# Half an item later: when the first network's side work reads another engine's result

## Chip, core and metric

The kernel runs on one core of a Trainium2 chip. The metric is device time in microseconds (us) of one execution. Before the change it is 1354.57 us, the median of three runs (1351.06, 1354.57 and 1358.54). The work of the core is done by five engines that run side by side and meet only where one waits for another: TensorE (PE, matmuls; PEld is its weight load), VectorE (DVE), ScalarE (ACT), GpSimd (POOL) and SyncE (SP), which issues most DMAs. Each engine takes its own instructions strictly in the order in which they were written for it.

## What is computed

A gated linear attention, then two feed-forward networks on 3072 tokens (4 batches x 768 positions):

```python
for t in range(S):                                  # q, k, v, alpha: [4, 8, 768, 48]
    state = alpha[:, :, t, :, None] * state + einsum('bhd,bhe->bhde', k[:, :, t], v[:, :, t])
    y[:, :, t] = einsum('bhd,bhde->bhe', q[:, :, t], state)
x = y as [3072, 384]
...
h = x @ w_in                                        # first network, 384 -> 2048 -> 384
x = where(h > 0, h, exp(min(h, 0)) - 1) @ w_out
...
p = domain_probs / (domain_probs.sum(-1) + 1e-9)    # second network, 4 experts, 384 -> 1024 -> 384
out = sum_e p[:, e] * (maximum(x @ w1[e], 0) @ w2[e])
```

## The kernel before

**Pieces.** The positions are cut into 6 chunks of 128; a chunk of all 4 batches gives 512 columns. A (chunk, batch) pair is an attention *unit*. Every fp32 operand of a big matmul is held as two fp32r parts, the rounded value ("hi", an ACT copy) and the rest ("lo", a DVE subtraction that reads hi); `split` makes both. A product is then three matmuls: hi·hi, hi·lo, lo·hi.

**First network.** It is a list of 96 *items* (chunk, slice of 128 hidden rows): the first 8 slices of chunk 0, all 16 of chunk 1, the other 8 of chunk 0, and then 16 each of chunks 2 to 5. Item i runs on the engines as

- `first` (9 matmuls, L420) into one of three PSUM banks h0 to h2, below "first matmuls of item i";
- `elu`: two ACT activations (L429, L430) and one DVE operation (L431), in place in the bank;
- `second` of item i-2 (9 matmuls, L446), which reads the parts `g` of item i-2;
- `parts`: an ACT copy (L436, below G0) and a DVE subtraction (L437, below G1). G1 is the last to read the bank, so the bank is free again only after it.

**Side work.** Beside the items run: the attention of the next chunk (steps of `unit_steps`: scores L250 and their mask L258, transposed keys L271 with an ACT copy L277, the prefix products P L205 and their inverse by logarithm and exponentials L213 to L215, Newton step L228 to L230, q times P L240, output L307/L314, state L341 with decay L351/L353); the way of the attention's output into the next chunk's x (`yout_t`'s `pack`: ACT copy L322, two DMAs to DRAM L324, one back L326, then `xtrans` splits it into x); the conversion of the first network's slices from 64-bit words (`conv_f64`: ACT multiply L406, three DVE bit operations L78, L81, L84, then a split into `w_W`); and the preparation of the second network's weights (`prep_w`: sums L474, splits into `wh`, DMAs to `wad` and `wbd`).

**What sets the order.** PE, ACT, DVE and POOL take the order in which the program writes them. `slots` puts steps behind the first matmuls of an item (half 0) or behind the second ones (half 1), `post` at the item's end. `later(f)` puts a follow-up (a mask, a lo part, a store) into a queue, and `flush` writes out what is in it:

```python
h = first(items[i])
self.flush()
... steps of half 0 ...
self.elu(h)
self.flush()
... second(items[i - 2]), steps of half 1, post ...
gs[items[i]] = self.parts(h)
```

Besides these two places, `do`, which runs each step, flushes the queue ahead of its step. SP's order is made by the scheduler. Two PSUM banks a0 and a1 serve the attention in turn: the scores of a unit need both, so they wait for the copy L322 and the decay L351 of the unit before, besides the DVE product L240.

Of the kernel before, what the change touches and what calls it, by code (L numbers as in the profile page):

```python
# [8 lines left out]
F32 = mybir.dt.float32  # L9
# [3 lines left out]
ALU = mybir.AluOpType  # L13
AX = mybir.AxisListType

B, H, S, D = 4, 8, 768, 48
# [72 lines left out]
class _Fast:  # L89
# [207 lines left out]
    def yout_t(self, u):  # L297


        nc = self.nc  # L300
        c, b = u
# [9 lines left out]
        for a in range(NP):  # L311
            for j in range(2):
                h = 2 * a + j
# [6 lines left out]
        def pack():  # L320
            y = self.ap.tile([128, NP * C], F32, tag="y", name="yt")
            nc.scalar.copy(y[0:SW], ps[0:SW])  # L322
            for j in range(2):
                nc.scalar.dma_start(out=self.x0d[b][D * j:D * (j + 1)], in_=y[64 * j:64 * j + D])  # L324
            x = self.ap.tile([128, KD, C], F32, tag="y", name="xr")
            nc.sync.dma_start(  # L326
                out=x, in_=self.x0d[b].rearrange("(k r) (a t) -> (r a) k t", k=KD, a=NP)
            )
            self.y[u] = x
# [67 lines left out]
    def conv_f64(self, f):  # L397
        nc = self.nc
# [9 lines left out]
        def bits():  # L408
            _f64_bits(nc, t, raw)
            self.split(w[:, 0, f % 2], w[:, 1, f % 2], tf)  # L410

# [21 lines left out]
    def parts(self, h):  # L433
        nc = self.nc
        g = self.hp.tile([128, 2, 512], F32R, tag="g", name="g")
        nc.scalar.copy(g[:, 0], h)  # L436
        nc.vector.tensor_tensor(out=g[:, 1], in0=h, in1=g[:, 0].bitcast(F32), op=ALU.subtract)  # L437
        return g
# [13 lines left out]
    def prep_w(self, g, nxt):  # L452
# [17 lines left out]
        def tile_w():  # L470
            return self.wp.tile([128, 3, 2, 128], F32R, tag="cv", name="wh", bufs=4)
# [4 lines left out]
        def end(c, q):  # L476
            t = tile_w()
            self.split(t[:, :, 0], t[:, :, 1], c)
            self.later(lambda: nc.sync.dma_start(out=self.wad[g][:, 3 * q:3 * q + 3], in_=t.bitcast(F32)))

# [4 lines left out]
        lo = lambda t, i, m=1: t[:, i:i + m] if m > 1 else t[:, i]  # L485
        tile_c = lambda: self.wp.tile([128, 3, 128], F32, tag="wc", name="wc", bufs=2)
        bc = lambda v, m: v.unsqueeze(1).to_broadcast([128, m, 128])
# [33 lines left out]
        def q4():  # L521
            t = tile_w()
            a = st[0][:, 1, 128:384].rearrange("p (n d) -> p n d", n=2)
            self.split(t[:, 0:2, 0], t[:, 0:2, 1], a)
            c = tile_c()
            tt(c[:, 0], w(1, 1), st["u"], sub)
            self.split(t[:, 2, 0], t[:, 2, 1], c[:, 0])
            self.later(lambda: nc.sync.dma_start(
                out=self.wbd[g][:, 0:768], in_=t.bitcast(F32).rearrange("p n h d -> p (n h d)")
            ))  # L530

# [10 lines left out]
        if nxt:  # L542
            s[5] += [nxt]
        return (load, (0,)), s
# [253 lines left out]
    def run(self):  # L798
# [22 lines left out]
        def do(step):  # L821
            if self.queue is not None:
                self.flush()
            for f, a in step:
                f(*a)
# [42 lines left out]
        for c in range(1, NCH):  # L868
# [3 lines left out]
            for n, s in enumerate(steps):  # L872
                k = av[n * len(av) // len(steps)]
                slots.setdefault(k, []).append(s)
                if n % 6 == 5:
                    slots[k].append([(load_next, ())])
            slots.setdefault((end - 1, 0), []).append([(self.xtrans, ((c, B - 1),))])

# [10 lines left out]
        for f in range(FS, F1):  # L889
            at((FS - 2, FS)[f - FS] if f < FS + 2 else f + 2, self.conv_f64, f)  # L890
            if f + 2 < F1:
                at(f + 2, self.load_f64, f + 2)
        b5 = n1 - F1
        at(b5 - 1, open_p2)
        at(FS + 4, self.load_probs)
# [7 lines left out]
        for n, s in enumerate(wsteps):  # L903
            at(w0 + n * (w1 - w0) // len(wsteps), do, s)
        for m in range(2):
# [45 lines left out]
        for i in range(n1):  # L951
# [10 lines left out]
            for f, a in post.pop(i, []):  # L962
                do([(f, a)])
            gs[items[i]] = self.parts(h)
        self.flush()
        self.queue = None
# [241 lines left out]
```

## Time and profile before

| | us |
|---|---|
| median of 3 runs | 1354.57 |
| profiled execution, its own time | 1352.57 |
| its span, first to last instruction | 1350.9 |
| PE busy | 1266.0 (94%) |
| DVE busy | 896.0 (66%) |
| ACT busy | 585.4 (43%) |
| POOL busy | 519.9 (38%) |
| mean granted TensorE clock | 0.974 |

The profiled execution lies 2.0 us below the median, and its own time is 1.7 us above its span. PE is the busiest engine, so what counts is where it is not busy or runs at less than its full clock. The page's 40 slices of the span show both at its start: PE is under nine tenths busy in six of the first nine slices (304 us), and its clock under nine tenths of full in five of the first seven (236 us); of the other 31 slices PE is under nine tenths busy in the last alone. The first network's items run from 42.5 to 602.6 us.

### The profile page before, as it was taken

To read this page: it belongs to the slowest core of one execution; us is meant where nothing else is said; L and a number is where in the kernel's file an instruction comes from. 1 tells how busy PE (TensorE), PEld (TensorE's weight loads), DVE (VectorE), ACT (ScalarE), POOL (GpSimd) and SP (SyncE) were. 2 spreads that over 40 slices of the span, in tenths; PEclk is the share of its full clock that TensorE was granted. 3 is DMA by queue.
4 is the path that set the end of the run, shared out by engine and by line. 5 is a ranking of instruction groups with operands and counts; after the bars stand their busy time and mean duration, and the time that the engine had idled before them with its cause. 6 is when DMAs were issued, how large, how long until landed. Compare 5 with 4: busy or idle time off the path is not lost.

```text
span 1350.9 us, 17707 instructions
## 1 busy us (share of the span) xinstructions
PE 1266.0 (94%) x6457; PEld 1022.5 (76%) x6457; DVE 896.0 (66%) x1513; ACT 585.4 (43%) x1076; POOL 519.9 (38%) x405
## 2 busy tenths in 40 slices
PE   8767979989999999999999999999999999999997
PEld 6546767767777778877887888778878878888886
DVE  7775676676667675656666675757676666667664
ACT  5444555555556655654434323243423332324231
POOL 0000000000000000457887664697865565547472
PEclk8788998999999999999999999999999999999999
DMA  5441424745466554682756546766463585434332
GB/s 218 170 152 65 140 92 174 234 158 199 141 208 196 190 181 156 213 294 91 278 195 229 179 176 215 296 254 251 163 258 123 198 314 179 168 129 169 127 102 77
DMA packets 71823, 248.28 MB, mean 184 GB/s; under 512 B 6712, under 2 KB 38296, under 8 KB 62384
## 3 DMA queue, kind: packets, MB, share of 16 engines
q1 hardware_dynamic: 68160, 237.62, 49.9%
q10 hardware_dynamic: 3568, 9.44, 1.9%
q8 instruction: 53, 0.87, 0.3%
q14 instruction: 42, 0.34, 0.1%
HBM read 182.89 MB, written 64.14 MB: 183 GB/s over the span
## 4 chain that ended last, share of the span: by engine, by line
PE 62%; DVE 15%; ACT 9%; issue 5%; POOL 4%; DMA 4%; ACTq 0%; SPq 0%; DVEq 0%; POOLq 0%
PE h L711 21%; PE t L761 12%; PE a L761 9%; PE h L420 7%; PE t L446 5%; PE h L761 4%; ACT g L436 2%; DVE P L205 2%; DVE u L731 2%; DVE h L431 1%; ACT wh L375 1%; DVE sm L258 1%; PE a L250 1%; ACT e L430 1%; DVE cv L84 1%
## 5 line engine op out<-in xcount | busy, mean ns | idle before, releaser
L420 PE MATMUL h<-x,w_W 128*128 128x512 f32 x864 | 228.3, 409 | 25.9 <-DVE g L437 16.6
L731 DVE TENSOR_TENSOR u<-h,u 128x512 f32<-128x512 f32 x258 | 177.5, 688 | 88.9 <-PE h L711 87.9
L446 PE MATMUL t<-g,w_W 128*128 128x512 f32 x864 | 219.3, 397 | 6.7 <-ACT g L436 3.5
L711 PE MATMUL h<-xc_Q,wa 128*128 128x512 f32 x780 | 219.4, 391 | 4.9 <-DVE c L731 2.4
L556 POOL TENSOR_TENSOR xs<-xr 128x512 f32<-128x512 f32 x8 | 10.3, 1294 | 544.1 <-ACT x1raw L937 544.1
L420 PEld LDWEIGHTS h<-x,w_W 128*128 128x128 f32 x864 | 167.4, 197 | 68.3 <-DVE g L437 20.0
L691 POOL TENSOR_TENSOR g_W<-c,g_W 128x512 fp32r<-128x512 f32 x128 | 164.8, 1303 | 121.8 <-ACT c L690 103.7
L689 ACT ACTIVATE g_W<-c 128x512 fp32r<-128x512 f32 x128 | 80.0, 626 | 272.0 <-DVE c L731 158.5
L446 PEld LDWEIGHTS t<-g,w_W 128*128 128x128 f32 x864 | 161.9, 190 | 46.0 <-DVE g L437 5.5
L711 PEld LDWEIGHTS h<-xc_Q,wa 128*128 128x128 f32 x780 | 145.6, 188 | 38.3 <-DVE u L731 4.3
L761 PE MATMUL t<-g_W,wb 128*128 128x512 f32 x576 | 157.6, 389 | 0.0
L437 DVE TENSOR_TENSOR g<-h,g 128x512 fp32r<-128x512 f32 x96 | 66.3, 691 | 89.8 <-ACT g L436 89.8
L761 PEld LDWEIGHTS t<-g_W,wb 128*128 128x128 f32 x576 | 108.0, 188 | 22.6 <-POOL g_W L691 0.2
L690 ACT ACTIVATE c<-c 128x512 f32<-128x512 f32 x192 | 121.1, 632 | 7.4
L731 DVE TENSOR_TENSOR c<-u,h 128x512 f32<-128x512 f32 x123 | 84.1, 686 | 50.3 <-PE h L711 37.1
L711 PE MATMUL h<-xc_W,wa 128*128 128x512 f32 x390 | 110.2, 391 | 5.1 <-DVE u L731 3.1
L725 DVE COPY u<-h 128x512 f32<-128x512 f32 x99 | 68.1, 691 | 66.7 <-PE h L711 66.4
L761 PE MATMUL a<-g_W,wb 128*128 128x512 f32 x384 | 111.7, 389 | 0.3 <-POOL g_W L691 0.3
L691 POOL TENSOR_TENSOR g_X<-c,g_X 128x512 fp32r<-128x512 f32 x64 | 82.7, 1304 | 62.6 <-ACT c L690 52.0
L689 ACT ACTIVATE g_X<-c 128x512 fp32r<-128x512 f32 x64 | 40.0, 626 | 142.5 <-DVE c L731 78.4
L431 DVE SCALAR_TENSOR_TENSOR h<-e,h 128x512 f32<-128x512 f32 x96 | 66.5, 693 | 44.6 <-ACT e L430 44.2
L711 PEld LDWEIGHTS h<-xc_W,wa 128*128 128x128 f32 x390 | 72.7, 188 | 22.6 <-DVE u L731 4.4
(139 smaller groups left out, 1948.1 us busy)
## 6 DMA issues: line engine op xcount, KB each, us to landing
wa<-wad SPq DMA_DIRECT2D x33, 1536.0 KB, 6.8
wb<-wbd SPq DMA_DIRECT2D x30, 1536.0 KB, 7.0
raw<-in_att_dram SPq DMA_DIRECT2D x22, 960.0 KB, 5.5
wad<-wh SPq DMA_DIRECT2D x44, 384.0 KB, 2.7
wbd<-wh SPq DMA_DIRECT2D x43, 384.0 KB, 3.4
xcd<-xh SPq DMA_DIRECT2D x30, 512.0 KB, 3.0
wraw<-in_wm_dram SPq DMA_DIRECT2D x16, 768.0 KB, 4.2
wraw<-in_we_dram SPq DMA_DIRECT2D x20, 576.0 KB, 4.6
```

What stands on the lines that cost most here:

```text
L205: nc.vector.tensor_tensor_scan(P[:, a, :], raw[:, A0 + a * C:A0 + (a + 1) * C], self.plo.to_broadcast([128, C]), 1.0, ALU.mult, ALU.max,)
L420: nc.tensor.matmul(h[:, 0:n], w[:, wl, fi, k * 128:(k + 1) * 128], x[:, xl, k, n0:n0 + n], start=(k == 0 and i == 0), stop=(k == KD - 1 an ...
L431: nc.vector.scalar_tensor_tensor(out=h, in0=e, scalar=-1.0, in1=h, op0=ALU.add, op1=ALU.max)
L437: nc.vector.tensor_tensor(out=g[:, 1], in0=h, in1=g[:, 0].bitcast(F32), op=ALU.subtract)
L446: nc.tensor.matmul(self.xa[k][:, 0:n], w[:, wl, fi, DM + k * 128:DM + (k + 1) * 128], g[:, gl, 0:n], start=(first and i == 0), stop=(last ...
L689: nc.scalar.activation(out=g[:, n, 0], in_=v, func=AF.Relu)
L690: nc.scalar.activation(out=v, in_=v, func=AF.Relu)
L691: nc.gpsimd.tensor_tensor(out=g[:, n, 1], in0=v, in1=g[:, n, 0].bitcast(F32), op=ALU.subtract)
L711: nc.tensor.matmul(b, w[:, wl], x[:, xl], start=(j == 0), stop=(j == 2))
L725: nc.vector.tensor_copy(out, b)
L731: (nc.vector if "b" in (a0, a1) or dst == "S5" else nc.gpsimd).tensor_tensor(out=out, in0=val(a0, b), in1=val(a1, b), op=ALU.add if op == ...
L761: nc.tensor.matmul(oa[m, d], wt[:, f, wl, d * 128:(d + 1) * 128], G[m][:, f, gl], start=first, stop=last)
```

## The change

Six edits, all in the first network's stretch and its side work:

1. `do` no longer flushes. Follow-ups now come out at two places in an item alone: behind its first matmuls and behind `elu`.
2. `parts` puts the G1 subtraction at the head of the queue, so it comes out behind the next item's first matmuls; nothing else stands on DVE between the old and the new place.
3. The splits of `conv_f64` and of `prep_w` (`end`, `q4`) go into the queue themselves, so that hi is written one flush behind the operation that makes its source, and lo one flush behind hi. The tiles `wc` have 4 buffers in place of 2.
4. The weight preparation's steps go into half items in place of item ends, and its next load one step later.
5. `xtrans` of a chunk's last unit goes half an item earlier.
6. The two stores of `pack` are issued by SP, not ACT.

```diff
@@ yout_t / pack
-                nc.scalar.dma_start(out=self.x0d[b][D * j:D * (j + 1)], in_=y[64 * j:64 * j + D])
+                nc.sync.dma_start(out=self.x0d[b][D * j:D * (j + 1)], in_=y[64 * j:64 * j + D])
@@ conv_f64
             _f64_bits(nc, t, raw)
-            self.split(w[:, 0, f % 2], w[:, 1, f % 2], tf)
+            self.later(lambda: self.split(w[:, 0, f % 2], w[:, 1, f % 2], tf))
@@ parts
         nc.scalar.copy(g[:, 0], h)
-        nc.vector.tensor_tensor(out=g[:, 1], in0=h, in1=g[:, 0].bitcast(F32), op=ALU.subtract)
+        self.queue.insert(
+            0, lambda: nc.vector.tensor_tensor(out=g[:, 1], in0=h, in1=g[:, 0].bitcast(F32), op=ALU.subtract)
+        )
@@ prep_w (end; q4 alike)
         def end(c, q):
-            t = tile_w()
-            self.split(t[:, :, 0], t[:, :, 1], c)
-            self.later(lambda: nc.sync.dma_start(out=self.wad[g][:, 3 * q:3 * q + 3], in_=t.bitcast(F32)))
+            def parts():
+                t = tile_w()
+                self.split(t[:, :, 0], t[:, :, 1], c)
+                self.later(lambda: nc.sync.dma_start(out=self.wad[g][:, 3 * q:3 * q + 3], in_=t.bitcast(F32)))
+
+            self.later(parts)
@@
-        tile_c = lambda: self.wp.tile([128, 3, 128], F32, tag="wc", name="wc", bufs=2)
+        tile_c = lambda: self.wp.tile([128, 3, 128], F32, tag="wc", name="wc", bufs=4)
@@
-            s[5] += [nxt]
+            s[6] += [nxt]
@@ run
         def do(step):
-            if self.queue is not None:
-                self.flush()
             for f, a in step:
                 f(*a)
@@
-            slots.setdefault((end - 1, 0), []).append([(self.xtrans, ((c, B - 1),))])
+            slots.setdefault((end - 2, 1), []).append([(self.xtrans, ((c, B - 1),))])
@@
-            at(w0 + n * (w1 - w0) // len(wsteps), do, s)
+            k = 2 * w0 + n * 2 * (w1 - w0) // len(wsteps)
+            slots.setdefault((k // 2, k % 2), []).append(s)
```

PE's order is the same before and after. The order of ACT and DVE is not; three places follow (line numbers of the changed file are up to 11 higher, and G1 is its L438).

ACT in items 0 and 1 (G0 is L436, `w_W` a converted slice, `yt` the packed output and `x0d` its DRAM copy). Before:

```order
L429 ACTIVATE e<-h_537 128x512
L430 ACTIVATE e<-e 128x512
L213 ACTIVATE lnP<-P 128x512
L214 ACTIVATE rP,pacc<-lnP 128x512
L215 ACTIVATE lnP,pacc<-lnP 128x512
L406 ACTIVATE cv<-wraw_484 128x768
L375 CAST w_W_525<-cv 128x768
L436 CAST g<-h_537 128x512
L322 COPY yt<-a_608 112x512
L324 DMA x0d_62<-yt 48x512 x2
L429 ACTIVATE e<-h_597 128x512
L430 ACTIVATE e<-e 128x512
```

And in the changed kernel:

```order
L213 ACTIVATE lnP<-P 128x512
L214 ACTIVATE rP,pacc<-lnP 128x512
L215 ACTIVATE lnP,pacc<-lnP 128x512
L406 ACTIVATE cv<-wraw_484 128x768
L436 CAST g<-h_537 128x512
L429 ACTIVATE e<-h_588 128x512
L430 ACTIVATE e<-e 128x512
L375 CAST w_W_525<-cv 128x768
L322 COPY yt<-a_606 112x512
L406 ACTIVATE cv<-wraw_532 128x768
L436 CAST g<-h_588 128x512
```

The hi copy of the slice that L406 has just begun stood ahead of item 0's G0 and stands now behind item 1's two activations; the two stores behind `yt` are gone from ACT.

DVE in item 14, one of those that convert slices with no attention beside them (L78, L81 and L84 are the three bit operations, L376 the lo part). Before:

```order
L431 SCALAR_TENSOR_TENSOR h_1281<-e,h_1281 128x512
L78 TENSOR_SCALAR cv<-cv 128x768
L81 SCALAR_TENSOR_TENSOR cv<-wraw_1239,cv 128x768
L84 SCALAR_TENSOR_TENSOR cv<-wraw_1239,cv 128x768
L437 TENSOR_TENSOR g<-h_1281,g 128x512
L376 TENSOR_TENSOR w_W_1306<-cv,w_W_1306 128x768
```

And in the changed kernel:

```order
L376 TENSOR_TENSOR w_W_1233<-cv,w_W_1233 128x768
L78 TENSOR_SCALAR cv<-cv 128x768
L81 SCALAR_TENSOR_TENSOR cv<-wraw_1204,cv 128x768
L84 SCALAR_TENSOR_TENSOR cv<-wraw_1204,cv 128x768
L431 SCALAR_TENSOR_TENSOR h_1275<-e,h_1275 128x512
L438 TENSOR_TENSOR g<-h_1275,g 128x512
```

The three bit operations moved from behind `elu`'s L431 to ahead of it.

ACT in items 35 and 36, in the attention's stretch with the weight preparation beside it (`kn` the transposed keys, `wc` and `wh` a weight sum and its parts). Before:

```order
L429 ACTIVATE e<-h_2401 128x512
L430 ACTIVATE e<-e 128x512
L277 COPY kn<-h_2423 128x512
L213 ACTIVATE lnP<-P 128x512
L214 ACTIVATE rP,pacc<-lnP 128x512
L215 ACTIVATE lnP,pacc<-lnP 128x512
L518 COPY wc<-wraw 128x128
L375 CAST wh<-wc 128x3x128
L436 CAST g<-h_2401 128x512
```

And in the changed kernel:

```order
L429 ACTIVATE e<-h_2396 128x512
L430 ACTIVATE e<-e 128x512
L277 COPY kn<-h_2421 128x512
L523 COPY wc<-wraw 128x128
L436 CAST g<-h_2396 128x512
L213 ACTIVATE lnP<-P 128x512
L214 ACTIVATE rP,pacc<-lnP 128x512
L215 ACTIVATE lnP,pacc<-lnP 128x512
L375 CAST wh<-wc 128x3x128
L429 ACTIVATE e<-h_2461 128x512
```

The three operations of the inverse and the hi copy stood between `elu` and G0 and stand now behind G0.

## Rows read from the trace of the kernel before

**Rows 1.** Windows by stretch: length, busy us per engine (instructions), PEclk, DMA share, GB/s.

```profile
42.50:125.10 82.60, 53.92 (x401) 42.22 (x399) 59.18 (x97) 38.93 (x70) 0.00 (x0) 0.85 0.40 139
125.10:182.40 57.30, 51.23 (x198) 39.72 (x199) 36.85 (x53) 29.17 (x47) 0.00 (x0) 0.92 0.35 112
182.40:545.00 362.60, 337.21 (x2146) 269.87 (x2145) 249.26 (x516) 205.19 (x423) 0.00 (x0) 0.98 0.53 178
...
602.60:1350.90 748.30, 729.98 (x3198) 598.00 (x3196) 483.60 (x720) 251.52 (x418) 483.25 (x370) 1.00 0.52 191
```

**Rows 2.** Timeline of PE: start, us, what, and in brackets idle time before.

```profile
60.24 2.08 PE L250 MATMUL a<-raw 48*128 48x128 f32 x16 [8.77 <-ACT e L430]
...
77.72 1.16 PE L250 MATMUL a<-raw 48*128 48x128 f32 x16 [2.82 <-ACT yt L322]
...
97.52 2.08 PE L250 MATMUL a<-raw 48*128 48x128 f32 x16 [6.86 <-ACT e L430]
...
122.76 0.79 PE L420 MATMUL h<-x,w_W 128*128 128x512 f32 x1 [4.13 <-ACT x L375]
125.11 3.78 PE L420 MATMUL h<-x,w_W 128*128 128x512 f32 x8 [1.55 <-DVE x L376]
...
298.11 3.92 PE L420 MATMUL h<-x,w_W 128*128 128x512 f32 x9 [3.33 <-DVE g L437]
```

**Rows 3.** Waits of PE from 182.4 to 545 us: total, times, longest.

```profile
PE h L420 <- DVE g L437: 12.2, 7, 3.3
PE a L250 <- ACT e L430: 6.9, 3, 2.5
PE h L420 <- DVE x L376: 3.4, 4, 1.8
PE a L250 <- issue: 2.7, 2, 2.2
```

**Rows 4.** Waits of DVE from 42 to 605 us, the longest.

```profile
DVE g L437 <- ACT g L436: 89.8, 83, 3.4
```

**Rows 5.** Timeline ahead of the scores at 60.24 us.

```profile
54.98 0.96 DVE L84 SCALAR_TENSOR_TENSOR cv<-wraw,cv 128x768 int32<-128x768 int32 x1
55.97 0.83 ACT L375 CAST w_W<-cv 128x768 fp32r<-128x768 f32 x1 [3.00 <-DVE cv L84]
...
57.81 1.02 ACTq L324 DMA_DIRECT2D x0d<-yt  x2
...
58.79 0.35 DVE L351 TENSOR_TENSOR tmp<-a,st 128x192 f32<-128x192 f32 x1
...
59.46 0.69 DVE L240 TENSOR_TENSOR raw<-raw,P 128x512 f32<-128x512 f32 x1
...
60.16 0.70 DVE L431 SCALAR_TENSOR_TENSOR h<-e,h 128x512 f32<-128x512 f32 x1
```

**Rows 6.** Timeline from one item that converts a slice into the next.

```profile
160.06 0.88 ACT L406 ACTIVATE cv<-wraw 128x768 f32<-128x768 f32 x1
...
161.09 0.56 DVE L78 TENSOR_SCALAR cv<-cv 128x768 int32<-128x768 int32 x1
...
163.66 0.83 ACT L375 CAST w_W<-cv 128x768 fp32r<-128x768 f32 x1 [2.73 <-DVE cv L84]
...
165.01 0.69 DVE L437 TENSOR_TENSOR g<-h,g 128x512 fp32r<-128x512 f32 x1 [1.38 <-ACT g L436]
...
165.62 0.95 DVE L376 TENSOR_TENSOR w_W<-cv,w_W 128x768 fp32r<-128x768 f32 x1
...
167.09 0.55 DVE L78 TENSOR_SCALAR cv<-cv 128x768 int32<-128x768 int32 x1
```

**Rows 7.** Timeline of item 35 ahead of the wait at 298.11 us.

```profile
294.37 0.28 DVE L474 TENSOR_TENSOR wc<-wraw 128x128 f32<-128x128 f32 x1
...
297.36 0.69 DVE L437 TENSOR_TENSOR g<-h,g 128x512 fp32r<-128x512 f32 x1 [2.71 <-ACT g L436]
```

**Rows 8.** Waits of SP's DMA queue: the load of `xr` for the stores.

```profile
SPq L326 <- DMA x0d<-yt: 90.7, 18, 7.3
```

More of the change, by code (lines that the diff above doesn't have):

```diff
@@ L521, in q4, with parts @@
         def q4():
-            t = tile_w()
             a = st[0][:, 1, 128:384].rearrange("p (n d) -> p n d", n=2)
-            self.split(t[:, 0:2, 0], t[:, 0:2, 1], a)
             c = tile_c()
             tt(c[:, 0], w(1, 1), st["u"], sub)
[L527 to L530, printed above, removed]
+            def parts():
+                t = tile_w()
+                self.split(t[:, 0:2, 0], t[:, 0:2, 1], a)
+                self.split(t[:, 2, 0], t[:, 2, 1], c[:, 0])
+                self.later(lambda: nc.sync.dma_start(
+                    out=self.wbd[g][:, 0:768], in_=t.bitcast(F32).rearrange("p n h d -> p (n h d)")
+                ))
+            self.later(parts)
         def w2(n):
@@ L893, in run @@
         b5 = n1 - F1
+        at(b5 - 1, self.flush)
         at(b5 - 1, open_p2)
@@ L962, in run @@
             for f, a in post.pop(i, []):
-                do([(f, a)])
+                f(*a)
             gs[items[i]] = self.parts(h)
-        self.flush()
+        while self.queue:
+            self.flush()
         self.queue = None
```

## Prediction

> **What bounds the kernel now.** I read the windows by stretch first [rows 1]. Behind 602.6 us PE is busy 729.98 of 748.30 us at full clock. The change gives this stretch the same work, so I price it at nothing. In the first network's stretch PE is not busy for 82.6 - 53.92 = 28.7 us up to 125.1 us (stretch A), 6.1 us up to 182.4 us (B) and 25.4 us up to 545 us (C). The granted clock is also below full there. With two levels, 1.2 and 2.4 GHz, a mean of 0.85 says 30% of A at the low one, 24.8 us; if PE had work in all of it, half, 12.4 us, was lost. For B 0.92 gives up to 4.6 us, for C 0.98 up to 7.3 us. Next I read PE's timeline and waits [rows 2, 3]. The long waits end at three things: scores that wait for q times P or for the banks of the unit before, first matmuls that wait for a bank which G1 has not freed, and first matmuls that wait for the next chunk's x. DVE and ACT end these waits, but they are not full: DVE is busy 249 of 363 us in C. They wait for each other. G1 alone waited 89.8 us for G0 [rows 4], because G0 stood on ACT behind work that waited for DVE. So PE is bound by the order of two half-idle engines, and the change edits that order.
>
> After a wait the clock can fall too: the nine matmuls behind the 3.33 us wait at 298.11 us took 3.92 us [rows 2], against 2.05 us for nine at the mean of the last stretch (729.98 / 3198 = 0.228 us each [rows 1]).
>
> **The change, stretch A (items 0 to 7): -15 us.** The chain ahead of the scores at 60.24 us [rows 5]: L84 ends at 55.94, the hi copy on ACT waits for it, G0 and G1 follow, then DVE's lo part, the decay at 58.79 and q times P at 59.46. From L84's end to the scores it is 4.3 us. In the new order hi is no longer ahead of G0, G1 runs before the bit operations, and behind L84 DVE has only q times P (0.69), L431 (0.70) and the decay's first operation (0.35): 1.75 us. G1 and its wait move ahead of L84, which I put 0.9 us later, so the scores start at about 56.8 + 1.75 = 58.5. I walked the rest of the stretch in the same way, with the orders of ACT and DVE in the changed kernel and these durations: scores of the next two units at about 71.6 and 89.4 (before 77.72 and 97.52), and the first matmuls on chunk 1 at 110.5 (before 122.76, and 125.11 for its second matmul [rows 2]). In this walk the earlier `xtrans` saves a piece, but x still comes last: the packed copy waits for the lo part of the x before it. That is 14.6 us. The stretch can't gain more than DVE's own work allows, 82.6 - 59.2 = 23.4 us [rows 1]; if only the first chain and the two waits for x (4.13 + 1.55) improve, it is 1.8 + 5.7 = 7.5 us. I take 15, nearer to the walk than to either end.
>
> **Stretch B (items 8 to 18): +1 us.** Here the change costs. An item that converts a slice now takes 6.0 us [rows 6]: bit operations 2.57 (161.09 to 163.66), hi and G0 1.35 (to 165.01), G1 0.61, lo and L431 1.47 (to the next L78 at 167.09). In the new order L431 runs beside hi and is off the loop, but the next slice's L406 (0.88) stands between hi and G0: 2.57 + 1.35 + 0.88 + 0.61 + 0.95 = 6.4 us. PE needs 18 x 0.228 = 4.1 us. Six such items follow each other; the lead of two items hides the first two or three. So 0.4 x 5 = +2 us, less 1 us for a start on a shorter wait. From below it is a gain of 3 us (the wait at its start and the low clock behind it go), from above a loss of 4 us (the normalisation of the probabilities falls into one of these items again, and nothing is hidden).
>
> **Stretch C (items 19 to 81): -24 us.** Four parts [rows 3].
> - x: 3.4 us in 4 waits, none over 1.84. `xtrans` goes one half item earlier, and its lo part is ahead of the next L431: half an item is 9 x 0.228 = 2.05 us. All 3.4 go.
> - Scores: 6.9 + 2.7 = 9.6 us in 5 waits. q times P stood behind a G1 whose G0 stood behind a hi copy and the two stores (1.02 us on ACT [rows 5]). Both are gone: 8 us. The decay and the copy L322 come half an item later, which eats the rest.
> - Banks: 12.2 us in 7 waits. In item 35 DVE was done with the weight sums at 294.65, and G1 started at 297.36, since ACT had the inverse, a copy and a hi copy ahead of G0 [rows 7]. In the new order G0 is ahead of the inverse, so of the 3.33 us wait 2.71 goes. I take three quarters of 12.2: 9 us.
> - Clock: 4 of the 7.3 us, as the longest waits are those that go.
>
> Together 24. From below x and the one worked wait, 3.4 + 2.7, and 2 us of clock: 8. From above all: 25.4 + 7.3 = 33.
>
> **At nothing.** The weight preparation's follow-ups come one or two half items later; nothing of the second network is loaded before 545 us. If a load for the next weight group came late, a sum L474 would hold DVE, at some 2 us a group. The G1 edit leaves G1's place on DVE. The move of the stores takes 40 issues, 20 x 1.02 us, off ACT; where ACT holds PE up, that is in the terms above. On SP they stand directly ahead of the load of `xr`, which has waited for the stores' landing before: 90.7 us in 18 waits, 5.0 us each [rows 8]. I leave that wait as it is. The Trainium skill ("DMA: Bandwidth & Descriptors", section "Two DMAs through the same engine are not ordered") says that two DMAs on one queue are not ordered by it and that the issuer must still wait for the first one's semaphore. If the queue did order them, the load could go 5.0 us earlier, and x at the end of A some 2 us sooner: 1313. By the rule it is the forecast below; no row here has both on one queue.
>
> Sum: -15 + 1 - 24 = -38 us on the profiled execution's 1352.6 us: 1314.6, so **1315 us**. That execution is 2.0 us under the median, within the 7.5 us between the runs; I don't add this.
>
> **Rivals.**
> 1. *DVE takes over.* The waits go from ACT, but DVE's order still has the bit operations, now ahead of L431, and the sums and masks ahead of G1. Then only the lower ends hold: -7.5 + 4 - 8 = -11.5, 1341 us. For it: DVE is busy 59 of 82.6 us in A. Against: 249 of 363 in C.
> 2. *Nothing moves on PE.* G0 gets earlier but what PE waits for stands behind other work on the same engine. 1352.6, within 0.5%. For it: ACT is busy in 205 of 363 us of C alone [rows 1], and most of its idle time costs nothing. Against: the walk of items 34 to 38, where each bank is free 1.6 us or more ahead of need.
> 3. *Slower: SP holds x back.* A weight load or store of `wad` stands between the stores and `xr` in several units of the new SP order. If it waits for a lo part that now comes one more half item later, `xr` is late, ACT blocks at the hi copy of x in front of G0, and PE waits. From the packed copy to that hi copy there are one to three items, an item being 362.6 / 63 = 5.8 us in C; the way through DRAM takes over 5 [rows 8]. If SP adds 5 us in the 16 units of stretch C and G1's lead takes 1.5, it is 16 x 3.5 = 56 us against a gain of 38: 1371. It decides from 38 / 16 = 2.4 us of PE's time a unit on. Against it: in the order the lo part in question is at most two items old.
>
> **Chances.** The forecast's case 0.70, DVE taking over 0.17, nothing 0.07, slower 0.06. The likeliest case reaches from 1301 (23 in A, 28 in C) to 1330 (10 and 14, +1); rival 1 takes the range to 1339. About 0.5%, 7 us, is what this kernel's runs can tell from no change: faster 0.87, within 0.07, slower 0.06.
>
> **What would show it.** The scores of units 2 to 4 at 58.5, 71.6 and 89 us, the first matmuls on chunk 1 near 110; items 13 to 18 at 6.4 us each with a wait of PE left there; G1's wait for G0 under 50 us; PE's waits from there to the end of the attention under 10 us; the second network unchanged in length at 748 us. It is wrong if ACT's hi copies of x wait for DMAs, or if DVE's busy share in A doesn't rise above 0.72.

## The result, and the profile after

The changed kernel takes 1301.24 us (median of four runs, 1299.45 to 1303.72); the kernel before takes 1352.82 us beside it (four runs, 1347.2 to 1358.54). The ratio is 0.962, with a 95% interval from 0.9575 to 0.9665: 51.6 us faster, where 38 were forecast. The profiled execution took 1303.72 us, with a span of 1302.0 us, 48.9 us under the span before.

From the page of the changed kernel, the busy times of the engines:

```profile
PE 1254.5 (96%) x6457; PEld 1018.2 (78%) x6457; DVE 896.6 (69%) x1513; ACT 585.6 (45%) x1076; POOL 521.4 (40%) x405
```

DVE, ACT and POOL do the work that they did. PE is busy 11.5 us less, for the same matmuls; it ran more of them at full clock.

To see where the 48.9 us lie I measure between marks that every kernel here has: the start of the first activation of `elu` (L429) in items 0, 8, 19, 82 and 95. Their rows in the kernel before, from ACT's timeline:

```profile
47.52 0.60 ACT L429 ACTIVATE e<-h 128x512 f32<-128x512 f32 x1
...
128.93 0.60 ACT L429 ACTIVATE e<-h 128x512 f32<-128x512 f32 x1 [3.71 <-PE h L420]
...
187.51 0.60 ACT L429 ACTIVATE e<-h 128x512 f32<-128x512 f32 x1
...
547.41 0.60 ACT L429 ACTIVATE e<-h 128x512 f32<-128x512 f32 x1
...
600.79 0.60 ACT L429 ACTIVATE e<-h 128x512 f32<-128x512 f32 x1 [1.47 <-PE h L420]
```

And in the changed kernel:

```profile
39.88 0.60 ACT L429 ACTIVATE e<-h 128x512 f32<-128x512 f32 x1 [2.06 <-PE h L420]
...
108.42 0.60 ACT L429 ACTIVATE e<-h 128x512 f32<-128x512 f32 x1
...
163.91 0.60 ACT L429 ACTIVATE e<-h 128x512 f32<-128x512 f32 x1
...
491.09 0.59 ACT L429 ACTIVATE e<-h 128x512 f32<-128x512 f32 x1
...
548.90 0.60 ACT L429 ACTIVATE e<-h 128x512 f32<-128x512 f32 x1 [1.47 <-PE h L420]
```

The differences of neighbouring marks, in us; A, B and C are the prediction's stretches, D is the one behind them, which it priced at nothing. The marks are ACT's, and PE does not stand at the same matmul at them before and after. So the column "by first matmuls" gives the change between the first matmuls of the same items on PE (for A and B the second matmul of item 8), on which the forecast's stretches stand:

| | before | after | change | by first matmuls | forecast |
|---|---|---|---|---|---|
| start to item 0 | 47.5 | 39.9 | -7.6 | -5.4 | 0 |
| A, items 0 to 8 | 81.4 | 68.5 | -12.9 | -14.9 | -15 |
| B, 8 to 19 | 58.6 | 55.5 | -3.1 | -5.5 | +1 |
| C, 19 to 82 | 359.9 | 327.2 | -32.7 | -31.0 | -24 |
| D, 82 to 95 | 53.4 | 57.8 | +4.4 | +4.9 | 0 |
| from item 95 to the end | 750.1 | 753.1 | +3.0 | +3.0 | 0 |
| sum | 1350.9 | 1302.0 | -48.9 | -48.9 | -38 |

The two columns differ at item 0 because its mark moved with the change. PE starts item 0 at 42.54 us before and at 37.14 after, and its nine matmuls take 2.70 and 2.71 us. But before, `elu` stood on ACT behind the hi copy of a slice, which waited 3.09 us for L84:

```profile
46.31 0.83 ACT L375 CAST w_W<-cv 128x768 fp32r<-128x768 f32 x1 [3.09 <-DVE cv L84]
```

From item 0's first matmul to its mark it was 4.98 us before and is 2.74 after. These 2.2 us are the change's, and in the forecast's count they belong to A.

The windows of the changed kernel over A and C, which answer to [rows 1]:

```profile
39.90:108.40 68.50, 53.25 (x399) 43.09 (x400) 54.12 (x92) 37.74 (x69) 0.00 (x0) 0.88 0.48 158
...
163.90:491.10 327.20, 324.28 (x2129) 263.26 (x2126) 245.28 (x517) 205.50 (x426) 4.02 (x3) 0.99 0.58 198
```

PE is idle 2.9 of 327.2 us in C (327.20 - 324.28). Before, between the same marks, it was busy 334.51 of 359.90 us:

```profile
187.50:547.40 359.90, 334.51 (x2135) 267.61 (x2134) 246.97 (x514) 204.71 (x424) 1.60 (x2) 0.98 0.53 181
```

So by the marks the 32.7 us of C are 22.5 us of idle time (25.4 - 2.9) and 10.2 us of busy time (334.51 - 324.28). Between the same first matmuls, before and after, the busy time falls by less:

```profile
182.38:544.43 362.05, 336.66 (x2144) 269.39 (x2142) 248.72 (x515) 204.62 (x422) 0.00 (x0) 0.98 0.53 178
156.53:487.62 331.09, 327.94 (x2143) 265.68 (x2142) 247.59 (x519) 207.13 (x425) 1.41 (x2) 0.99 0.58 197
```

That is 22.2 us of idle and 8.7 us of busy time. The clock accounts for 6.8 us of it. Read in short windows, the granted clock is 0.50, the lower level, for 17.1 us of C before, in five places that each follow a wait of PE of 2.0 to 3.3 us, and for 3.4 us after. PE is busy throughout them, so half of the 13.7 us of difference, as the lower level is half the higher, is the loss that is gone. The other 1.9 us of busy time stay open.

What is left of PE's waits in C (answers to [rows 3]) is all that view lists there:

```profile
PE a L250 <- ACT yt L322: 0.7, 1, 0.7
PE a L250 <- DVE tmp L351: 0.7, 1, 0.7
PE h L420 <- DVE x L376: 0.5, 1, 0.5
PE a L250 <- issue: 0.4, 1, 0.4
PE t L448 <- DVE x1part L944: 0.4, 1, 0.4
PE h L271 <- DVE g L438: 0.2, 1, 0.2
```

The 12.2 us in which first matmuls waited for G1 are gone, and so are the 9.6 us of scores but for 1.8. In A PE still waits; the rows of its timeline that answer to [rows 2]:

```profile
52.23 2.19 PE L250 MATMUL a<-raw 48*128 48x128 f32 x16 [5.55 <-ACT yt L322]
...
65.13 1.25 PE L250 MATMUL a<-raw 48*128 48x128 f32 x16
...
82.53 2.19 PE L250 MATMUL a<-raw 48*128 48x128 f32 x16 [6.71 <-ACT yt L322]
...
104.77 1.46 PE L420 MATMUL h<-x,w_W 128*128 128x512 f32 x3 [1.95 <-DVE x L376]
```

### The profile page after: what moved, and what is told of

It is laid out like the page before. It is cut to its first block, busy times and chain, and to the rows that moved or that the text cites. A ratio compares the mean times of both kernels' runs of the same rounds, so it can differ in the third digit from the quotient of the medians.

```text
span 1302.0 us, 17669 instructions
## 1 busy us (share of the span) xinstructions
PE 1254.5 (96%) x6457; PEld 1018.2 (78%) x6457; DVE 896.6 (69%) x1513; ACT 585.6 (45%) x1076; POOL 521.4 (40%) x405
## 3 DMA queue, kind: packets, MB, share of 16 engines
q1 hardware_dynamic: 70720, 241.56, 52.6%
## 4 chain that ended last, share of the span: by engine, by line
PE 75%; DVE 9%; ACT 5%; DMA 4%; issue 3%; POOL 3%; SPq 0%; DVEq 0%; ACTq 0%; POOLq 0%
PE h L720 22%; PE t L770 13%; PE h L420 11%; PE t L448 10%; PE a L770 9%; PE h L770 4%; DMA x0d<-yt 2%; PE a L250 1%; DVE u L740 1%; PE a L307 1%; PE a L314 1%; DMA xr<-x0d 1%; DVE wh L376 1%; POOL g_W L700 1%; DVE c L789 1%
## 5 line engine op out<-in xcount | busy, mean ns | idle before, releaser
L420 PE MATMUL h<-x,w_W 128*128 128x512 f32 x864 | 219.2, 398 | 3.1 <-DVE x L376 2.4
L420 PEld LDWEIGHTS h<-x,w_W 128*128 128x128 f32 x864 | 163.1, 191 | 40.0 <-DVE x L376 3.6
L431 DVE SCALAR_TENSOR_TENSOR h<-e,h 128x512 f32<-128x512 f32 x96 | 66.5, 693 | 75.1 <-ACT e L430 75.0
L734 DVE COPY u<-h 128x512 f32<-128x512 f32 x99 | 68.1, 690 | 68.5 <-PE h L720 66.7
L700 POOL TENSOR_TENSOR g_X<-c,g_X 128x512 fp32r<-128x512 f32 x64 | 82.5, 1301 | 63.1 <-ACT c L699 52.4
L438 DVE TENSOR_TENSOR g<-h,g 128x512 fp32r<-128x512 f32 x96 | 65.9, 686 | 49.1 <-ACT g L436 48.9
```

The lines of the kernel that those rows point to most:

```text
L420: nc.tensor.matmul(h[:, 0:n], w[:, wl, fi, k * 128:(k + 1) * 128], x[:, xl, k, n0:n0 + n], start=(k == 0 and i == 0), stop=(k == KD - 1 an ...
L431: nc.vector.scalar_tensor_tensor(out=h, in0=e, scalar=-1.0, in1=h, op0=ALU.add, op1=ALU.max)
L438: 0, lambda: nc.vector.tensor_tensor(out=g[:, 1], in0=h, in1=g[:, 0].bitcast(F32), op=ALU.subtract)
L700: nc.gpsimd.tensor_tensor(out=g[:, n, 1], in0=v, in1=g[:, n, 0].bitcast(F32), op=ALU.subtract)
L734: nc.vector.tensor_copy(out, b)
```

## The experiments

**The theory** after the result: the gain is made by the distance between a result and the instruction on another engine that reads it. With hi queued (edit 3) and the queue written out at two places of an item (edit 1), ACT stands far less at a hi copy waiting for DVE while G0, on which DVE waits, is behind it. **The rivals**: the 40 issues taken off ACT (edit 6), the earlier `xtrans` (edit 5), the spreading of the weight steps (edit 4). Edit 2 has no run of its own: by the program nothing is written on DVE between its old and its new place.

Each run was timed five or six times against the kernel before, whose median was 1353.6, 1354.4 and 1353.07 us beside the three sets of four. Stretches are measured between the same marks, in one profiled execution each:

| | median, us | ratio to before (95%) | start | A | B | C | D |
|---|---|---|---|---|---|---|---|
| before | | | 47.5 | 81.4 | 58.6 | 359.9 | 53.4 |
| changed kernel | 1301.24 | 0.962 (0.9575-0.9665) | 39.9 | 68.5 | 55.5 | 327.2 | 57.8 |
| undo_weight_splits | 1333.28 | 0.9847 (0.981-0.9884) | 42.3 | 67.8 | 55.5 | 358.8 | 57.6 |
| undo_slice_splits | 1316.79 | 0.9718 (0.9683-0.9753) | 41.9 | 75.2 | 64.8 | 326.3 | 57.9 |
| undo_stores | 1301.54 | 0.9613 (0.9576-0.9649) | 40.1 | 66.2 | 55.5 | 327.6 | 56.8 |
| undo_do_flush | 1316.16 | 0.9728 (0.9692-0.9764) | 44.0 | 71.0 | 54.5 | 339.5 | 52.9 |
| edits_1_and_3 | 1308.21 | 0.9657 (0.9637-0.9677) | 41.9 | 67.2 | 56.0 | 334.8 | 54.7 |
| undo_xtrans | 1305.75 | 0.965 (0.9628-0.9672) | 41.9 | 68.4 | 55.3 | 328.7 | 58.5 |
| undo_weight_slots | 1303.37 | 0.9635 (0.9612-0.9658) | 39.7 | 68.2 | 55.5 | 329.5 | 54.7 |
| half_items_g0_first | 1291.3 | 0.956 (0.9532-0.9587) | 39.7 | 65.4 | 52.8 | 326.7 | 53.8 |
| weights_done_by_item_80 | 1304.08 | 0.9649 (0.9619-0.968) | 40.1 | 68.5 | 55.5 | 332.3 | 52.6 |
| both_together | 1298.93 | 0.9594 (0.9568-0.962) | 42.0 | 67.2 | 52.8 | 332.8 | 52.6 |
| g0_first_copy_first | 1291.58 | 0.9548 (0.9522-0.9574) | 40.8 | 65.3 | 52.8 | 325.7 | 53.9 |
| g0_first_bits_later | 1298.86 | 0.9597 (0.9571-0.9624) | 42.3 | 67.4 | 58.6 | 325.5 | 53.9 |

**1. The weights' splits.**

```diff
@@ prep_w, end and q4 (changed kernel -> this)
-            self.later(parts)
+            parts()
```

> The changed kernel, but the parts of the second network's weights (end, q4) are again split at once, so that hi stands on ACT directly behind the sum that DVE makes for it, often ahead of G0 (four of the five splits of a group). Theory (the gain of stretch C comes from clearing G0's way): up to item 19 as in the changed kernel; from there to the 82nd item most of the bank term comes back, 6 to 9 us, PE waits for G1 over 5 us there (changed kernel 1.3), G1's wait for G0 rises from 48.9 to about 65; 1308 to 1311 us. Rival (the stores or the places of the flush give the gain of C): within 3 us of 1301.

32 us slower than the changed kernel, and C alone is 31.6 us longer: it is back within 1.1 us of the kernel before, with PE idle 24.4 us and busy 334.40 us there (by first matmuls it is 359.4 us, against 362.1 before and 331.1 in the changed kernel):

```profile
165.50:524.30 358.80, 334.40 (x2132) 268.45 (x2131) 246.37 (x518) 204.03 (x426) 3.98 (x3) 0.97 0.52 182
```

The theory has the right stretch, but the size is four times what I had put on it. What ACT waited for DVE's sums at the weights' hi copies in C, in the kernel before, the changed kernel and this run:

```profile
ACT wh L375 <- DVE wc L474: 50.7, 26, 5.6
```

```profile
ACT wh L375 <- DVE wc L476: 15.9, 16, 1.7
```

```profile
ACT wh L375 <- DVE wc L476: 64.9, 27, 5.8
```

It is more in this run than in the kernel before, which may come of the weight steps' half items, which the kernel before lacks. So the run shows that C's gain needs the queued splits; it does not show that they would give all of it by themselves. The timeline shows one such place, with DVE's last sum, the hi copy behind it, G0 and G1:

```profile
298.82 0.62 DVE L476 TENSOR_TENSOR wc<-wc,wraw 128x128 f32<-128x128 f32 x2
299.47 0.51 ACT L375 CAST wh<-wc 128x384 fp32r<-128x384 f32 x1 [4.29 <-DVE wc L476]
...
299.89 0.58 ACT L436 CAST g<-h 128x512 fp32r<-128x512 f32 x1
...
300.37 0.59 ACT L322 COPY yt<-a 112x512 f32<-112x512 f32 x1
300.50 0.69 DVE L438 TENSOR_TENSOR g<-h,g 128x512 fp32r<-128x512 f32 x1 [1.07 <-ACT g L436]
```

ACT stands idle for 4.29 us, and all that is behind the hi copy is late by it, not G0 alone: the packed copy L322 too, on which scores and x depend. I had taken only the banks' waits to come back, and of those 5.2 us did. In C, the scores' come back as well (they add up to 12.1 us under six names), then x's (1.3), and the lower clock with them: 18.6 us of C against 3.4, a loss of some 7 us.

**2. The slices' splits.**

```diff
@@ conv_f64 / bits (changed kernel -> this)
-            self.later(lambda: self.split(w[:, 0, f % 2], w[:, 1, f % 2], tf))
+            self.split(w[:, 0, f % 2], w[:, 1, f % 2], tf)
```

> The changed kernel, but conv_f64 splits its slice again directly behind the three bit operations, so that hi stands on ACT ahead of elu's two activations and waits for L84 there. Theory (hi behind a DVE result is what made stretches A and B slow): an item that converts a slice becomes a loop of G1 0.69, bits 2.57, hi 0.83, activations 1.2, L431 0.70, G0 0.59 and L406 0.88 = 7.5 us against 6.2; stretch B 6 to 8 us longer, A 5 to 10 us longer, C unchanged: 1312 to 1319 us. Rival (in A and B the order of G1 and the earlier x give the gain, the hi copy is beside the path): within 4 us of 1301.

As the theory said: 15.6 us slower, A 6.7 and B 9.3 us longer, C unchanged. The loop of a converting item is shorter than I had added up (L78 follows L78 after 6.67 us, not 7.5), since L406 runs on ACT while DVE is at L431. With the first experiment this parts the gain by stretch: without edit 3 in `prep_w` that of C goes, without edit 3 in `conv_f64` a part of A's, and B gets slower than before. The other five edits were in place in both.

**3. The stores.**

```diff
@@ yout_t / pack (changed kernel -> this)
-                nc.sync.dma_start(out=self.x0d[b][D * j:D * (j + 1)], in_=y[64 * j:64 * j + D])
+                nc.scalar.dma_start(out=self.x0d[b][D * j:D * (j + 1)], in_=y[64 * j:64 * j + D])
```

> The changed kernel, but the two stores of pack are issued by ACT again, behind the packed copy. Theory (the gain is in the split orders): 20 x 1.02 us come back on ACT, mostly in its idle time; 1301 to 1305 us, PE's waits in stretch C under 6 us. Rival (of the scores' term of 8 us most was the stores): 1307 to 1311, PE's waits for scores in stretch C back above 5 us.

Nothing: 1301.54 against 1301.24 us. ACT has the time. What the move does change is SP's wait for the stores' landing ahead of the load of `xr`, which answers to [rows 8]. First this run, then the changed kernel:

```profile
SPq L326 <- DMA x0d<-yt: 89.3, 20, 7.8
```

```profile
SPq L326 <- DMA x0d<-yt: 42.6, 19, 5.9
```

It halves, without PE noticing. It does not vanish, although store and load are now on one queue: 2.2 us each. So the program still waits for the landing of the stores. That is what the Trainium skill asks for ("DMA: Bandwidth & Descriptors", section "Two DMAs through the same engine are not ordered"); no run here leaves the wait out, so what the queue alone would do is not shown.

**4. The places of the flush.**

```diff
@@ do (changed kernel -> this; post alike)
         def do(step):
+            if self.queue is not None:
+                self.flush()
             for f, a in step:
```

> The changed kernel, but do flushes the queue again ahead of every step, so that a follow-up comes out up to four times in an item, and hi and lo of a split one step, not half an item, behind their source. Theory (the distance of half an item is what pays): half of the gain goes, in A and C alike, 1315 to 1335 us, G1's wait for G0 above 65 us. Rival (that the splits are queued at all is enough, the distance does not matter): within 5 us of 1301.

14.9 us slower, at the near end of the expectation. By the marks C is 12.3 us longer; by first matmuls A is 3.3, B 5.1 and C 8.8 us longer. The distance counts, not the queue alone. Item 0's mark comes 4.98 us behind its first matmul again, as in the kernel before. But the sign that I gave was wrong: G1 waited 32.1 us for G0 here, less than the 48.9 us of the faster kernel. Of D this run is 4.9 us shorter; see 6.

**5. Edits 1 and 3 alone, and edits 4 and 5 taken back one by one.** The first is the kernel before with edits 1 and 3 as in the diff ahead. The others:

```diff
@@ undo_xtrans
-            slots.setdefault((end - 2, 1), []).append([(self.xtrans, ((c, B - 1),))])
+            slots.setdefault((end - 1, 0), []).append([(self.xtrans, ((c, B - 1),))])
@@ undo_weight_slots (and the next load at s[5])
-            k = 2 * w0 + n * 2 * (w1 - w0) // len(wsteps)
-            slots.setdefault((k // 2, k % 2), []).append(s)
+            at(w0 + n * (w1 - w0) // len(wsteps), do, s)
```

> The kernel before with edits 1 and 3 alone: do no longer flushes, and the splits of the slices and of the weights are queued (wc has 4 buffers). The stores stay on ACT, G1 in parts, xtrans and the weight steps at their old places. Theory (the gain is the distance between a result and its reading, and these two edits make all of it): first activation of elu from item 0 to 8 in 68 to 72 us (before 81.4, changed 68.5), 8 to 19 in 55 to 57 (58.6, 55.5), 19 to 82 in 327 to 331 (359.9, 327.2); 1300 to 1306 us. Rival (the weight steps in half items and the earlier xtrans carry a good part): 19 to 82 in 338 us or more, 1312 to 1325.

> The changed kernel with xtrans of a chunk's last unit back at its old place, half an item later. Theory (x would be late again at each of the five chunk borders: in the run with edits 1 and 3 alone PE waited 5.7 us in 5 waits for x's lo part L376): PE's waits for x at L420 rise from 2.9 to 7 us or more, items 19 to 82 in 330 to 332 us (327.2); 1304 to 1307 us. Rival (that run's late x came from the weight steps at item ends, in front of x's split): within 2 us of 1301, waits for x under 4 us.

> The changed kernel with the weight steps back at the items' ends (and the next load at its old step). Theory (half items spread two steps that fell on one place, and keep the second half's sums out of G0's way): of the 7.6 us by which items 19 to 82 take longer with edits 1 and 3 alone, 3 to 5 us stand here: 330 to 332 us; items 82 to 95 near 55; 1302 to 1306 us. Rival (all 7.6 us are x's): items 19 to 82 in 327 to 328.

Two edits of six make 25.1 of the 32.7 us of C, and A and B but for run to run differences; 1308.21 us lies 2 us above the theory's range and 4 below the rival's. Of the 7.6 us that they lack in C, the runs with one edit taken back show 1.5 (the half item of `xtrans`), 2.3 (the half items of the weight steps) and 0.4 us (the stores). By first matmuls the same three are 2.2, 2.1 and 2.3 us, so one profile each does not tell them apart, and the rest belongs to no single edit. What the half items of the weight steps win in C they lose in D: 54.7 us without them, 57.8 with them. The waits of PE for x were expected at 7 us without the earlier `xtrans` and came to 4.1 in all (3.4 for the lo part, 0.7 for hi), against 2.9: a miss of the theory. Both kernels are near 1301 in the median (4.5 and 2.1 us above), and their intervals overlap with the changed kernel's; the stretches say more than the medians here.

**6. Stretch D.**

```diff
@@ weights_done_by_item_80 (changed kernel -> this)
-WPREP = (20, 92)
+WPREP = (20, 80)
```

> The changed kernel, but the weight preparation ends with item 80, not 92, so that its lo subtractions no longer run on DVE beside POOL's sums and splits. Theory (these lo parts took 0.99 and 1.27 us there against 0.72 in the kernel before, since POOL runs beside them, and G1 behind them was late): lo parts back to 0.75 us or less, no wait of PE for G1 behind item 82, items 82 to 95 in 52 to 54 us (57.8), 19 to 82 within 3 us of 327.2; 1296 to 1299 us. Rival 1 (the follow-ups' place, not POOL, makes the wait): items 82 to 95 short, but the waits for G1 stand in C, which is 4 us or more longer; 1301 to 1306. Rival 2 (the wait in D has another cause): 82 to 95 stays at 57 us or more.

D falls from 57.8 to 52.6 us, as the theory has it, but C rises from 327.2 to 332.3 us, so the time is no better. No wait for G1 stands in C, so rival 1 has the place wrong and the sum right: the denser steps make DVE late with the partial x (2.0 us) and with the decay.

D's 4.4 us are 3.0 us more idle time of PE (0.4 before, 3.4 after) and 1.4 us of busy time; 3.4 us of it ran at the lower clock, none before. What was wrong in D, in the changed kernel's timeline ahead of its longest wait there:

```profile
529.87 1.29 POOL L376 TENSOR_TENSOR xc_W<-xs,xc_W 128x512 fp32r<-128x512 f32 x1
529.91 1.53 DVE L376 TENSOR_TENSOR wh<-wraw,wh 128x256 fp32r<-128x256 f32 x1
...
531.12 2.75 POOL L565 TENSOR_TENSOR xs<-xr 128x512 f32<-128x512 f32 x2
531.36 1.38 DVE L376 TENSOR_TENSOR wh<-wc,wh 128x128 fp32r<-128x128 f32 x1
...
532.66 1.61 DVE L376 TENSOR_TENSOR wh<-wraw,wh 128x384 fp32r<-128x384 f32 x1
...
534.20 0.68 DVE L438 TENSOR_TENSOR g<-h,g 128x512 fp32r<-128x512 f32 x1
...
534.93 2.39 PE L448 MATMUL t<-g,w_W 128*128 128x512 f32 x5 [2.50 <-DVE g L438]
535.37 1.28 POOL L376 TENSOR_TENSOR xc_W<-xs,xc_W 128x512 fp32r<-128x512 f32 x1
535.40 1.67 DVE L376 TENSOR_TENSOR wh<-wraw,wh 128x384 fp32r<-128x384 f32 x1
```

And in the run with the weights done by item 80, DVE's groups of the same three shapes in items where POOL has nothing to do (mean ns of one behind the comma):

```profile
L376 DVE TENSOR_TENSOR wh<-wraw,wh 128x384 fp32r<-128x384 f32 x2 | 1.1, 550 | 0.0
...
L376 DVE TENSOR_TENSOR wh<-wraw,wh 128x256 fp32r<-128x256 f32 x1 | 0.4, 419 | 0.0
L376 DVE TENSOR_TENSOR wh<-wc,wh 128x128 fp32r<-128x128 f32 x1 | 0.3, 285 | 0.0
```

The three lo parts ahead of G1 take 1.53, 1.38 and 1.61 us beside POOL's sums and splits, and 0.42, 0.29 and 0.55 us without them: 3.3 us longer, and PE waits 2.50 us. G1 itself, which reads its bank, takes 0.68 us either way. The Trainium skill ("GPSIMD Engine Reference", section "8. Key points") says that GpSimd shares its interfaces to SBUF with VectorE and contends with instructions that have two SBUF inputs. The trace agrees: the lo parts have two and get longer, G1 has one and a bank and does not.

**7. G0 ahead of the item's end.**

```diff
@@ run (changed kernel -> this)
+            gs[items[i]] = self.parts(h)
             for f, a in post.pop(i, []):
                 f(*a)
-            gs[items[i]] = self.parts(h)
```

> The changed kernel, but G0 is written ahead of what stands at the item's end, so that the next slice's L406 is behind G0 on ACT. Theory (stretch B is the loop bits, hi, L406, G0, G1, lo): the period of converting items falls from 6.18 by 0.88 to about 5.3 us, items 8 to 19 from 55.5 to 51 to 53 us, the rest unchanged: 1297 to 1299 us. Rival (B is bound by DVE's lo and bits alone, or by the lead of two items): no change, within 1 us of 1301.

> The changed kernel with G0 ahead of the item's end and the weight preparation done by item 80. If the two stretches are independent, the two gains add: 1293 to 1297 us. If the denser weight steps need the slack that G0's old place gave, it is no faster than the better of the two.

The best version of the study, together with g0_first_copy_first below: 1291.3 us, 10 us under the changed kernel and below the range expected. One line takes L406 out of the loop of the converting items. DVE's L78 in two successive ones, in the changed kernel and here:

```profile
134.31 0.55 DVE L78 TENSOR_SCALAR cv<-cv 128x768 int32<-128x768 int32 x1
...
140.49 0.55 DVE L78 TENSOR_SCALAR cv<-cv 128x768 int32<-128x768 int32 x1
```

```profile
130.62 0.55 DVE L78 TENSOR_SCALAR cv<-cv 128x768 int32<-128x768 int32 x1
...
136.02 0.55 DVE L78 TENSOR_SCALAR cv<-cv 128x768 int32<-128x768 int32 x1
```

6.18 us become 5.40 us; B is 2.7 us shorter, as expected. D is 4.0 us shorter, which I had not expected: G0 stood there behind what is written at the items' ends as well. The lo parts beside POOL are no shorter in this D (1.44 us in the mean for the 128x384 ones of `wraw`, against 1.27 in the changed kernel), but PE's waits for G1 fall from 3.4 to 1.1 us. So a longer lo part costs PE time only where PE needs the G1 behind it. Together with the earlier weights (1298.93 us) the gains do not add: C's loss of 5 to 6 us comes along, and D is only 1.2 us better.

**8. What is left in A.** In stretch A of half_items_g0_first scores still wait 10.4 us, put down to the packed copy L322.

```diff
@@ g0_first_copy_first (half_items_g0_first -> this; decay alike, outside the items as before)
-        self.later(pack)
+            self.queue.insert(0, pack)
@@ g0_first_bits_later (g0_first_copy_first -> this)
-        self.later(bits)
+        self.later(lambda: self.later(bits))
```

> half_items_g0_first, with the packed copy L322 and the decay at the head of the queue, so that L322 no longer stands behind the slice's hi copy on ACT. If the two scores' waits at 51.2 and 80.9 us (10.4 us, put down to L322) are L322's, the scores start some 0.8 us earlier or more each: items 0 to 8 in 61 to 64 us (65.4). If they are DVE's (bits, q times P, L431 and the decay's L351 follow each other to 51.30, and L351 must end too), nothing changes: 65 to 66, 1291 us.

> g0_first_copy_first, with the three bit operations one flush later, behind elu's L431 and the decay. Theory (DVE's 2.5 us of bits stand ahead of q times P and the decay, on which the scores wait): the scores' waits in items 0 to 8 fall from 10.4 to about 5 us; items 0 to 8 in 60 to 63 us; items 8 to 19 lose 0 to 3 us, as G1 now stands behind the bits; 1286 to 1293 us. Rival (DVE is the bound of items 0 to 8 whatever the order, 62 of 68 us busy): waits move to x or to the banks, items 0 to 8 stay at 65 or more, and with B's loss 1292 to 1298 us.

With the copy moved ahead the scores start a little sooner and end no sooner:

```profile
47.73 0.57 ACT L322 COPY yt<-a 112x512 f32<-112x512 f32 x1
...
50.87 0.68 DVE L240 TENSOR_TENSOR raw<-raw,P 128x512 f32<-128x512 f32 x1
...
51.66 2.89 PE L250 MATMUL a<-raw 48*128 48x128 f32 x16 [4.05 <-issue]
```

L322 ends at 48.30, q times P at 51.55, and the scores follow that, 10.9 us behind item 0's mark. In half_items_g0_first L322 ended at 51.19 and they followed at 51.24, 11.6 us behind it. So the copy, 4.0 us earlier by the marks, brings 0.7 us and no more, since DVE's product was the wait just behind it. The scores now take 2.89 us in place of 2.19, in part since all but the first two of their weight loads wait 0.42 us for the decay, and A stays (65.3 against 65.4 us). The view had named the last of several waits. With the bits later the scores' waits fall further, from 9.0 to 5.8 us, but first matmuls in A now wait 7.1 us for the slices' parts, and in B second matmuls wait 5.2 us for G1. A is 2.1 and B 5.8 us longer: the rival's case, 0.9 us above its range. Its "62 of 68 us busy" is not what the trace shows: DVE is busy 54.1 of A's 65.3 us in g0_first_copy_first, and 54.12 of 68.5 us in the changed kernel. It seems that reordering DVE there only chooses who waits; that is argued, not shown.

## Why the prediction was right, and where its terms were off

The direction and the mechanism were right: waits of ACT for DVE in front of G0, taken out by distance. That the time lies within the range is luck: 1301.24 us is 0.2 us inside its lower end. B and C both gained more than the forecast's case allowed them, and the stretches priced at nothing nearly cancel (by first matmuls -5.4 at the start, +4.9 in D and +3.0 in the last stretch, 2.5 us in all).

- **Stretch A, -15 forecast.** Right: -14.9 by the first matmuls, on which the forecast's numbers stand (42.54 to 125.11 before, 37.14 to 104.77 after). Counted from the start of item 0, which is 5.4 us earlier, the scores of units 2 to 4 stand in the old kernel's time at 57.6, 70.5 and 87.9 us (forecast 58.5, 71.6, 89.4) and the second matmul on chunk 1 at 110.2 (110.5).
- **Stretch B, +1 forecast.** This term failed in sign: -5.5 by the first matmuls, beyond the gain of 3 us that was its bound, and -3.1 by the marks. The loop was forecast at 6.4 us and took 6.18, against 6.0 before, so the step itself is nearly right. What failed is what it was set against: the lead of the items hides more of the loop than I allowed. Before, PE waited 5.5 us for G0 and G1 in the items that convert slices, at four of them; now 2.8 us, at two. The wait at the start of the stretch, of whose shortening I had expected 1 us, did not shorten (1.55 before, 1.95 after). That the loop is a cost was shown by its shortening with L406 out of it, 2.7 us.
- **Stretch C, -24 forecast.** -31.0 by the first matmuls, -32.7 by the marks, beyond the 28 of the likeliest case. Waits: 20 forecast, 22 measured. The clock: 4 forecast, 6.8 measured, by the windows at its lower level. I had worked the clock's loss out from a printed mean of 0.98, as 7.3 us at most, and then taken half of it; it was 8.5 us (17.1 us at the lower level), and all of it hung on the waits. Some 2 us of busy time I had not seen and can't explain. What made the waits go was put down to three causes, stores, `xtrans` and hi copies. The runs show one in the main: with the weights' splits back, nearly everything comes back, and edits 1 and 3 alone make 25.1 us. The move of the stores, part of the 8 us for the scores, is worth nothing that the time shows.
- **D at nothing.** +4.4. I named a late load as the danger; it was DVE's lo parts beside POOL, nearly five times as long as alone at the worst, ahead of G1. In the kernel before, the lo parts of 128x384 took 0.72 us (of the sums) and 0.73 us (of `wraw`) in the mean there, in the changed kernel 1.14 and 1.27 us (an expectation above has 0.99 for the first): in their new places more of them run beside POOL.
- **The start, -7.6, and the last stretch, +3.0.** Of the first, 2.2 us are the change's, at item 0's mark, and the forecast's count has them in A; the other 5.4 us lie ahead of anything that the change edits (last section). The last stretch is longer with a lower clock: it took 753.1 us at a granted clock of 0.989, against 750.1 at 0.997 before, and its PE was busy 3.9 us longer. Over the fourteen profiles it took between 748.3 us (at 0.998) and 753.4 us (at 0.994), in the main more where the clock was lower. No run gives it to an edit.
- **The signs.** One of the two signs of being wrong came: ACT's hi copies of x now wait for DMAs, 12.5 us in 6 waits up to 4.8, where none did before. In C PE doesn't notice; at the end of A the longest of them stands ahead of the first matmuls on chunk 1, which wait 0.5 and 1.95 us. The other did not: DVE's busy share in A is 54.12 / 68.5 = 0.79 (over 0.72). G1's wait for G0 is 48.3 us from item 0 to 95 (under 50), but it is lower in a slower kernel, so it shows nothing. PE's waits in C are 2.9 us (under 10), the second network 753.1 us from item 95 on, against 750.1.
- **The rivals.** DVE takes over: it does in A and in D, and not beyond. Its own sum was 1341 us, while the stated range ended at 1339. Nothing moves: no. SP holds x back: ACT does block at hi copies of x, as this rival has it, but SP's wait for the stores got shorter, and PE's waits for x fell from 3.4 to 0.5 us in C.

## What to carry to other kernels

On engines that run strictly in order, write the reader of another engine's result half a loop step behind it, and the operation that frees a resource first. Look for the one instruction at which an engine stands still: what it costs is everything queued behind it, and the low clock behind some of the waits on top (behind five of PE's nine waits of 1 us or more in C of the kernel before), not only the wait that the profile names. When work is moved later, see which engine it then runs beside.

## What the runs showed of the chip

**The clock at the start.** From 12 to 24 us six of the fourteen profiled kernels ran at a granted clock of 0.72, five at 1.00, two at 0.91 and 0.86, and the kernel before at 0.60. The changed kernel, and undo_xtrans:

```profile
12.00:24.00 12.00, 10.87 (x117) 8.94 (x118) 11.96 (x25) 7.82 (x15) 0.00 (x0) 1.00 0.53 183
```

```profile
12.00:24.00 12.00, 10.89 (x78) 8.78 (x80) 10.22 (x20) 5.90 (x12) 0.00 (x0) 0.72 0.43 161
```

PE is busy as long in both and issues 117 matmuls in the one and 78 in the other. Item 0's first matmul, ahead of which all fourteen run the same matmuls and the same ACT and DVE operations, starts at 36.9 to 37.4 us at 1.00, and at 39.0 to 39.5 us at 0.72. So 0.72 costs some 2 us. The kernel before, at 0.60, starts it at 42.54: 5.4 us behind the changed kernel, in the same direction. With one profile of it, at a clock that none of the others had, the size stays open.

**DVE beside POOL.** A subtraction of 128x128 fp32 from SBUF took 1.38 us beside POOL and 0.29 us alone; one of 128x384 that began 0.03 us behind a POOL operation of 1.28 us (the last two rows of D's timeline) took 1.67 us and ended 0.42 us past POOL's end; alone it takes 0.55. It looks as if DVE waited until POOL was done; that was not measured by itself.
